# Block attention and two feed-forward stages in fp32 on one core: scores in all four quarters of TensorE, and three parts of w3 @ w_out behind the first x @ w_in

## The chip, the core and the metric

The kernel runs on one core of a Trainium2 chip. A core has TensorE (PE, with its weight loads PEld), VectorE (DVE), ScalarE (ACT), GpSimd (POOL) and SyncE (SP), which here only issues DMAs. The metric is the device time of one execution in microseconds; the number given is the median of several runs. One further execution was taken with the hardware profiler; all rows below are from it.

## What is computed

```python
# attention: batch 2, 8 heads, 768 positions, head size 64; block 32, window 16
k_sum = k.reshape(B, H, nb, block, D).max(axis=3)
v_sum = v.reshape(B, H, nb, block, D).mean(axis=3)
scores_l = where(|i - j| < window, scale * q @ k.T, -1e9)
scores_s = scale * q @ k_sum.T + log(block)
a = softmax(concat([scores_l, scores_s]))
x = a @ concat([v, v_sum])            # then as 1536 x 512
# first feed-forward stage: 512 -> 2048 -> 512
h = x @ w_in
x2 = (h - tanh(h)) @ w_out
# second stage: 512 -> 1024 -> 1024 -> 512
out = (((x2 @ w1) * (x2 @ w2)) @ w3) @ w_out2
```

All inputs and the output are fp32. The weights arrive on the chip as 64-bit numbers.

## The kernel before

**Precision and weights.** The products of the two feed-forward stages are made of three matmuls each (`split_mm`, L176 to L179: high x high, then two with a low half), with operands split into a high and a low half. Class `Weights` (L60) turns each 128x512 block of 64-bit weights ("unit") into such halves: a load by SP (L83), an activation by ScalarE (`start`, L99), three VectorE operations (L102, L104, L106; `dve` issues one of them, `unit` what is left of a unit), a cast by ScalarE (`high`, L134) and a subtraction by GpSimd (`low`, L141). At most three units are between start and `low`. During attention the three VectorE operations work on a PSUM tile `bits` (two buffers), later on the SBUF tile `dec`. Halves live in 15 places that are handed on when a unit has been used up. The matrix w3 @ w_out2 is computed once (32 `w34_part`s of six matmuls, L235; `w34_end`, L250, copies two sums of eight parts from PSUM to SBUF), so that the last stage multiplies by one matrix.

**Attention (L255 to L480).** A head pair (two heads on partitions 0 to 63 and 64 to 127) has 12 tiles of 64 queries; four tiles make a group, three groups a head pair, 24 groups in all. The order on all engines is written by hand: a loop over g = 0 to 27 issues work of up to five groups at once ("iteration g"). `scores(g + 1)` are eight fp32 matmuls 64x64 by 120 columns into one PSUM tile (two buffers). The two heads of a tile go to different halves of rows and of columns. `softmax_a(g, i)` is one VectorE reduction that adds the mask and takes the maximum (L341) and one ScalarE exponential (L344), per tile; `softmax_b(g - 1)` are two small VectorE operations and one GpSimd scaling (L351); `transposes(g - 2)` (L358) go to one PSUM bank, `probs(g - 2)` (L363) copies it to SBUF; `values(g - 3)` (L373) writes one PSUM bank `av`; `x_high(g - 4)` (L384) and `x_low(g - 4)` (L182) read it into the halves of x. `key_blocks` takes the maxima over key blocks on VectorE, and GpSimd writes them between the keys (L299). `value_blocks` (L310) makes the block means of a head pair; SP spreads them by DMA (L320). `busy` (L390) are products of the identity with itself that go nowhere. The number of `w34_part`s in each iteration stands in `N34` (L48). Iterations in `MORE` start two units instead of one.

TensorE's order in one iteration before: scores(g + 1), first part, transposes(g - 2), other parts, values(g - 3). VectorE's: the four reductions, with softmax_b behind the second, x_low behind the third and one decode operation behind each but the first; then a second unit, if one was started, and the key maxima. ScalarE's: x_high, copies of block means, casts of weights, four exponentials, the activation of the next unit, probs, copies of w34_end.

PSUM has eight banks. Attention uses two for scores, two for `bits`, one for transposes, one for `av` and two (`psw`) for w3 @ w_out2.

**First feed-forward stage (L607 to L626).** The loop over n = 0 to 49 issues `hidden(n)` (x @ w_in, 12 matmuls into bank n % 3), then decode work and `curve(n)` (h - tanh(h): for step n - 1 a VectorE select, L517, and ScalarE's cast and GpSimd's subtraction that give gh and gl; for step n four ScalarE and three VectorE operations), then `back(n - 2)` (12 matmuls with w_out into four banks). VectorE does the unit of the step between the select and the products of the curve. The loop before it (`while n34 < 32`) has nothing left to do here. The second stage (L653 on) is untouched.

```python
            for g in range(NG + 4):
...
                if g + 1 < NG:
                    scores(g + 1)
                for i in parts[:1]:
                    w34_part(i)
                if 0 <= g - 2 < NG:
                    transposes(g - 2)
                for i in parts[1:]:
                    w34_part(i)
...
                if 0 <= g - 3 < NG:
                    rest = values(g - 3)
```

Of the kernel before, what the change touches and what calls it, by code (L numbers as in the profile page):

```python
# [19 lines left out]
P = 128  # L20
# [13 lines left out]
TU = 4  # L34
# [13 lines left out]
N34 = [0, 0, 0, 0, 1, 1, 0, 1, 1, 0, 1, 1, 0, 1, 1] + [2] * 13  # L48
# [7 lines left out]
def fused_kernel(tc, qT, kT, vN, vW, w_in, w_out, w1, w2, w3, wo2, out):  # L56
# [3 lines left out]
    class Weights:  # L60
# [26 lines left out]
        def start(self, k=1):  # L87

            for _ in range(k):
# [8 lines left out]
                size = t if self.psum is None else self.psum.tile([P, 512], F32, tag="bits", bufs=2, name=f"bits_{n}")  # L98
# [87 lines left out]
    with tc.tile_pool(name="base", bufs=1) as base, \  # L186
# [68 lines left out]
        with tc.tile_pool(name="p1", bufs=1) as p1, \  # L255
# [66 lines left out]

            def scores(g):
                n, u = divmod(g, NU)
                ps = ps1.tile([P, TU, NC], F32, tag="s", bufs=2, name=f"s_{g}")
                for i in range(TU):
                    t = u * TU + i
                    for hf in range(2):
                        r = slice(hf * QT, (hf + 1) * QT)
                        mm(out=ps[r, i, :], lhsT=qt[n][r, t * QT:(t + 1) * QT], rhs=kt[n][r, t * CW:t * CW + NC],  # L330
                           start=True, stop=True)
                st[g] = ps

            def softmax_a(g, i):
                t = g % NU * TU + i
                mk = masks[0 if t == 0 else 2 if t == NQ - 1 else 1]
                if i == 0:
# [4 lines left out]
                    out=pr[g][:, i, :], in0=st[g][:, i, :], in1=mk[:, :], scale=-0.125, scalar=3.0e38,  # L342
# [23 lines left out]
            def values(g):  # L366
# [3 lines left out]
                for i in range(TU):  # L370
                    for hf in range(2):
                        r = slice(hf * QT, (hf + 1) * QT)
                        mm(out=av[r, i * QT:(i + 1) * QT], lhsT=vg[n][:NC, u * TU + i, r], rhs=sb[:, i, r],  # L373
# [22 lines left out]
            busy(8)  # L396
# [13 lines left out]
            for g in range(NG + 4):  # L410
# [14 lines left out]

                if g + 1 < NG:
                    scores(g + 1)
                for i in parts[:1]:
                    w34_part(i)
                if 0 <= g - 2 < NG:  # L430
                    transposes(g - 2)
                for i in parts[1:]:
                    w34_part(i)
# [17 lines left out]
                for i in range(TU):  # L451
                    if g < NG:
                        softmax_a(g, i)
# [19 lines left out]
            while n34 < 32:  # L473
                wt.start()
                wt.unit()
                w34_part(n34)
                w34_end(n34)
                n34 += 1
                wt.high()
                wt.low()  # L480
        w34_pools.close()
# [3 lines left out]
        psp = ctx.enter_context(tc.tile_pool(name="ps2", bufs=1, space=PSUM, reuse_waits="tile"))  # L485
# [6 lines left out]
        def bank(i, name):  # L492
            return psp.tile([P, TB], F32, tag=f"b{i}", name=name)
# [113 lines left out]
        for n in range(NS + LAG):  # L607
            nxt = hidden(n) if n < NS else None
            if n == NS:
# [12 lines left out]
            wt.low()  # L622
            if not closing:
# [103 lines left out]
```

## Time and profile before

| what | us |
|---|---|
| median of 3 runs | 605.48 |
| lowest and highest run | 603.28, 610.76 |
| the profiled execution | 600.9 |
| its span, first to last instruction | 599.1 |

The mean granted clock of TensorE over the span is 0.995 of full speed. Times in rows are in us from the start of the span unless marked ns. A row of the timeline has the start, the length, the engine, the line, the operation, output<-input with shapes, and how many instructions; in brackets the idle time of the engine before it and what ended that. A row of the busy time by stage has, for each engine, its busy us and the count of instructions, then TensorE's granted clock, the share of the DMA engines and GB/s. Matmuls overlap: a row's length contains the latency of its last matmul, so the time that a group takes is the distance from its start to the start of the next.

### The profile page before, as it was taken

Reading aid. Unit: us, or ns where it says so; the run is one execution under the profiler, and the core shown is the slowest. Engines: PE = TensorE matmul, PEld = TensorE weight load, DVE = VectorE, ACT = ScalarE, POOL = GpSimd, SP = SyncE. Lnnn points to the kernel's source line nnn. Section 1 sums busy time; section 2 is a strip of 40 time slices with the busy share of each in tenths; the row PEclk is TensorE's granted clock in tenths of the full one; section 3 lists DMA queues with packets and bytes.
Section 4 is the critical chain, followed back from the end, with each engine's and each line's share of the span. In section 5 each row is a group of like instructions: output and inputs, shape, how many; then the busy total and the mean of one; then the engine's idle time right before and its main releaser. Section 6 shows DMA issues by size and latency. Waiting matters only on the chain.

```text
span 599.1 us, 8969 instructions
## 1 busy us (share of the span) xinstructions
PE 580.5 (97%) x3216; PEld 469.1 (78%) x3216; DVE 391.8 (65%) x770; ACT 331.3 (55%) x728; POOL 248.0 (41%) x213
## 2 busy tenths in 40 slices
PE   8888999998999999999999999999899999999997
PEld 5666777776888888888888888878688888888885
DVE  3799987799999986679999879999500100010001
ACT  3699887777878864577766667744311211121111
POOL 3466555555566452235555324565632111111110
PEclk9999999998999999999999999999999999999999
DMA  8999986552322320022323002321000100010001
GB/s 310 332 324 321 346 293 207 158 166 105 106 94 85 106 69 0 1 69 73 103 74 106 2 0 73 104 75 67 1 0 1 70 1 0 1 70 1 0 2 70
DMA packets 19676, 59.69 MB, mean 100 GB/s; under 512 B 2096, under 2 KB 4784, under 8 KB 19632
## 3 DMA queue, kind: packets, MB, share of 16 engines
q1 hardware_dynamic: 19632, 59.12, 29.6%
q8 instruction: 25, 0.41, 0.3%
q14 instruction: 19, 0.16, 0.1%
HBM read 54.79 MB, written 3.15 MB: 97 GB/s over the span
## 4 chain that ended last, share of the span: by engine, by line
PE 75%; DVE 13%; issue 4%; DMA 4%; ACT 2%; POOL 1%; SPq 0%; ACTq 0%; DVEq 0%; POOLq 0%
PE x L178 6%; PE x L177 6%; PE x L179 6%; PE ph L177 6%; PE ph L179 6%; PE ph L178 6%; PE w L177 6%; PE w L178 6%; PE w L179 6%; PE o L179 3%; PE o L178 3%; PE o L177 3%; PE busy L394 2%; DVE dec L104 2%; DVE dec L106 2%
## 5 line engine op out<-in xcount | busy, mean ns | idle before, releaser
L141 POOL TENSOR_TENSOR wl<-dec,wh 128x512 fp32r<-128x512 f32 x72 | 111.5, 1552 | 50.2 <-ACT wh L134 43.9
L182 POOL TENSOR_TENSOR gl<-g,gh 128x512 fp32r<-128x512 f32 x48 | 65.1, 1357 | 140.3 <-ACT gh L527 82.3
L590 DVE TENSOR_TENSOR u_a<-u_a,w 128x512 f32<-128x512 f32 x24 | 16.5, 686 | 139.6 <-PE w L179 139.6
L182 POOL TENSOR_TENSOR gl_c<-u_a,gh_c 128x512 fp32r<-128x512 f32 x24 | 31.0, 1290 | 126.9 <-ACT gh_c L592 126.9
L177 PE MATMUL x<-gh,wh 128*128 128x512 f32 x192 | 75.6, 394 | 1.8 <-ACT gh L527 1.8
L178 PE MATMUL x<-gl,wh 128*128 128x512 f32 x192 | 75.7, 394 | 1.6 <-POOL gl L182 1.6
L179 PE MATMUL x<-gh,wl 128*128 128x512 f32 x192 | 75.3, 392 | 0.0
L177 PE MATMUL w<-xh,wh 128*128 128x512 f32 x192 | 75.0, 391 | 0.0
L178 PE MATMUL w<-xl,wh 128*128 128x512 f32 x192 | 75.0, 391 | 0.0
L177 PE MATMUL ph<-xh,wh 128*128 128x512 f32 x192 | 74.8, 390 | 0.0
L179 PE MATMUL w<-xh,wl 128*128 128x512 f32 x192 | 74.7, 389 | 0.0
L179 PE MATMUL ph<-xh,wl 128*128 128x512 f32 x192 | 74.7, 389 | 0.0
L178 PE MATMUL ph<-xl,wh 128*128 128x512 f32 x192 | 74.7, 389 | 0.0
L106 DVE SCALAR_TENSOR_TENSOR dec<-raw,dec 128x512 uint32<-128x512 uint32 x45 | 63.5, 1412 | 1.5
L522 ACT ACTIVATE u<-ph 128x512 f32<-128x512 f32 x48 | 28.8, 600 | 53.1 <-PE ph L179 53.1
L586 ACT COPY u_a<-w 128x512 f32<-128x512 f32 x24 | 14.0, 584 | 73.3 <-PE w L179 73.3
L592 ACT CAST gh_c<-u_a 128x512 fp32r<-128x512 f32 x24 | 14.9, 620 | 71.3 <-DVE u_a L590 71.3
L134 ACT CAST wh<-dec 128x512 fp32r<-128x512 f32 x72 | 44.3, 623 | 12.7 <-DVE dec L106 12.6
L532 DVE TENSOR_TENSOR g<-ph,u 128x512 f32<-128x512 f32 x48 | 32.8, 683 | 19.5 <-ACT th L523 19.4
L517 DVE COPY_PREDICATED g<-mk,th 128x512 f32<-128x512 uint32 x48 | 41.7, 870 | 4.0
L177 PEld LDWEIGHTS x<-gh,wh 128*128 128x128 f32 x192 | 36.3, 189 | 10.2 <-ACT gh L527 2.2
L178 PEld LDWEIGHTS x<-gl,wh 128*128 128x128 f32 x192 | 36.4, 190 | 9.9 <-POOL gl L182 2.3
(90 smaller groups left out, 1270.3 us busy)
## 6 DMA issues: line engine op xcount, KB each, us to landing
raw<-w SPq DMA_DIRECT2D x32, 512.0 KB
raw<-w_in SPq DMA_DIRECT2D x16, 512.0 KB
raw<-w_out SPq DMA_DIRECT2D x16, 512.0 KB
vg<-vW SPq DMA_DIRECT2D x8, 768.0 KB
raw<-wo SPq DMA_DIRECT2D x8, 512.0 KB
kt<-kT SPq DMA_DIRECT2D x7, 544.0 KB
vn<-vN SPq DMA_DIRECT2D x8, 384.0 KB
qt<-qT SPq DMA_DIRECT2D x7, 384.0 KB
```

Source lines behind the costliest of these rows:

```text
L106: lambda tu=tu, su=su, lo=lo: stt(out=tu, in0=lo, scalar=29, in1=su, op0=ALU.logical_shift_right, op1=ALU.bitwise_or)])
L134: nc.scalar.copy(out=h, in_=self.t[n])
L141: nc.gpsimd.tensor_tensor(out=l, in0=self.t[self.n_low], in1=h[:, :].bitcast(F32), op=ALU.subtract)
L177: mm(out=acc, lhsT=lh, rhs=rh, start=start, stop=False)
L178: mm(out=acc, lhsT=lh, rhs=rl, start=False, stop=False)
L179: mm(out=acc, lhsT=ll, rhs=rh, start=False, stop=stop)
L182: eng.tensor_tensor(out=out, in0=x, in1=high.bitcast(F32), op=ALU.subtract)
L517: nc.vector.copy_predicated(out=g, mask=mask[:, :].bitcast(U32), data=t)
L522: nc.scalar.activation(out=u, in_=ph, func=AF.Square)
L532: nc.vector.tensor_tensor(out=gn, in0=ph, in1=u, op=ALU.mult)
L590: nc.vector.tensor_tensor(out=a, in0=a, in1=pb, op=ALU.mult)
L592: nc.scalar.copy(out=ch, in_=a)
```

## The change

The PSUM tile of a group of scores becomes two tiles of half the size, one for the even and one for the odd query tiles, with three buffers. In odd tiles the two heads exchange the output partitions, so that the four matmuls of two neighbouring tiles go to four different quarters of TensorE; `values` reads the probabilities accordingly. The reductions and exponentials go in the order 0, 2, 1, 3. `bits` has one buffer; a second unit started in the same iteration is decoded in SBUF. TensorE's order in an iteration becomes: transposes, all parts, scores, values. Iterations 25 to 27 have 1, 0 and 0 parts (before 2, 2 and 0), and parts 29 to 31 follow `hidden(0)`; their sums are copied after `curve(1)`, and only then is the pool of their two banks closed. These two are banks 2 and 7 of the feed-forward stage. The first run of `busy` has four products instead of eight.

```diff
-N34 = [0, 0, 0, 0, 1, 1, 0, 1, 1, 0, 1, 1, 0, 1, 1] + [2] * 13
+N34 = [0, 0, 0, 0, 1, 1, 0, 1, 1, 0, 1, 1, 0, 1, 1] + [2] * 10 + [1, 0, 0]
...
         def start(self, k=1):
 
-            for _ in range(k):
+            for i in range(k):
...
-                size = t if self.psum is None else self.psum.tile([P, 512], F32, tag="bits", bufs=2, name=f"bits_{n}")
+                size = t if self.psum is None or i else self.psum.tile([P, 512], F32, tag="bits", bufs=1, name=f"bits_{n}")
...
+            def half_of(i, hf):
+
+                hf = (hf + i) % 2
+                return slice(hf * QT, (hf + 1) * QT)
+
             def scores(g):
+
                 n, u = divmod(g, NU)
-                ps = ps1.tile([P, TU, NC], F32, tag="s", bufs=2, name=f"s_{g}")
+                st[g] = [ps1.tile([P, TU // 2, NC], F32, tag="s", bufs=3, name=f"s_{g}_{z}") for z in range(2)]
                 for i in range(TU):
                     t = u * TU + i
                     for hf in range(2):
                         r = slice(hf * QT, (hf + 1) * QT)
-                        mm(out=ps[r, i, :], lhsT=qt[n][r, t * QT:(t + 1) * QT], rhs=kt[n][r, t * CW:t * CW + NC],
-                           start=True, stop=True)
-                st[g] = ps
+                        mm(out=st[g][i % 2][half_of(i, hf), i // 2, :], lhsT=qt[n][r, t * QT:(t + 1) * QT],
+                           rhs=kt[n][r, t * CW:t * CW + NC], start=True, stop=True)
...
-                if i == 0:
+                if g not in nm:
...
-                    out=pr[g][:, i, :], in0=st[g][:, i, :], in1=mk[:, :], scale=-0.125, scalar=3.0e38,
+                    out=pr[g][:, i, :], in0=st[g][i % 2][:, i // 2, :], in1=mk[:, :], scale=-0.125, scalar=3.0e38,
...
-                        mm(out=av[r, i * QT:(i + 1) * QT], lhsT=vg[n][:NC, u * TU + i, r], rhs=sb[:, i, r],
+                        mm(out=av[r, i * QT:(i + 1) * QT], lhsT=vg[n][:NC, u * TU + i, r], rhs=sb[:, i, half_of(i, hf)],
...
-            busy(8)
+            busy(4)
...
+                if 0 <= g - 2 < NG:
+                    transposes(g - 2)
+                for i in parts:
+                    w34_part(i)
                 if g + 1 < NG:
                     scores(g + 1)
-                for i in parts[:1]:
-                    w34_part(i)
-                if 0 <= g - 2 < NG:
-                    transposes(g - 2)
-                for i in parts[1:]:
-                    w34_part(i)
...
-                        softmax_a(g, i)
+                        softmax_a(g, (0, 2, 1, 3)[i])
...
-            while n34 < 32:
-                wt.start()
-                wt.unit()
-                w34_part(n34)
-                w34_end(n34)
-                n34 += 1
-                wt.high()
-                wt.low()
-        w34_pools.close()
...
-        psp = ctx.enter_context(tc.tile_pool(name="ps2", bufs=1, space=PSUM, reuse_waits="tile"))
+        psp = [ctx.enter_context(tc.tile_pool(name="ps2", bufs=1, space=PSUM, reuse_waits="tile"))] * 8
...
-            return psp.tile([P, TB], F32, tag=f"b{i}", name=name)
+            return psp[i].tile([P, TB], F32, tag=f"b{i}", name=name)
...
             nxt = hidden(n) if n < NS else None
+            if n == 0:
+                for i in range(n34, 32):
+                    w34_part(i)
...
             cur = curve(n, nxt, cur)
             wt.low()
+            if n == 1:
+                for i in range(n34, 32):
+                    w34_end(i)
+                w34_pools.close()
+                psp[2] = psp[7] = ctx.enter_context(tc.tile_pool(name="ps3", bufs=1, space=PSUM, side="right",
+                                                                 reuse_waits="tile"))
```

## Rows read from the trace of the kernel before

**Rows 1.** The page's first part: busy us, share and instructions of each engine.

```profile
PE 580.5 (97%) x3216; PEld 469.1 (78%) x3216; DVE 391.8 (65%) x770; ACT 331.3 (55%) x728; POOL 248.0 (41%) x213
```

**Rows 2.** Busy time by stage: start:end, length, then each engine in turn.

```profile
23.00:35.00 12.00, 10.36 (x140) 8.06 (x136) 11.30 (x51) 11.13 (x40) 7.12 (x7) 1.00 0.97 342
69.00:85.00 16.00, 15.66 (x160) 12.13 (x156) 14.29 (x55) 12.69 (x42) 8.40 (x8) 1.00 0.89 291
127.30:137.50 10.20, 8.43 (x39) 6.66 (x37) 9.96 (x14) 7.75 (x16) 3.73 (x3) 1.00 0.56 186
137.50:142.90 5.40, 4.39 (x12) 3.22 (x13) 5.23 (x8) 4.05 (x8) 3.16 (x3) 0.70 0.28 97
148.00:200.00 52.00, 52.00 (x231) 43.06 (x230) 50.42 (x68) 42.17 (x75) 31.04 (x20) 1.00 0.29 93
```

**Rows 3.** TensorE's timeline in iterations 18 and 19.

```profile
89.41 0.69 PE L373 MATMUL av<-pt,vg 120*64 120x64 f32 x16
90.03 0.64 PE L310 MATMUL av<-vn,mean 128*32 128x128 f32 x12
90.59 1.04 PE L330 MATMUL s<-kt,qt 64*64 64x120 f32 x16
91.56 0.50 PE L177 MATMUL w34a<-wh,wh 128*128 128x512 f32 x1
...
93.06 0.60 PE L358 MATMUL t<-ident,pr 128*120 128x128 f32 x4
```

**Rows 4.** TensorE's timeline at the start: busy products, scores 0 and 1, busy products.

```profile
1.36 6.77 PE L394 MATMUL busy<-ident 128*128 128x128 f32 x16 [1.36 <-POOL ident masks.py:199]
8.05 2.77 PE L330 MATMUL s<-kt,qt 64*64 64x120 f32 x32
10.75 4.32 PE L394 MATMUL busy<-ident 128*128 128x128 f32 x16
```

**Rows 5.** Timeline of GpSimd's key blocks and of VectorE's first reductions that waited.

```profile
5.30 0.42 POOL L299 COPY kt<-kb 128x288 f32<-128x288 f32 x1 [0.21 <-DVE kb L298]
10.09 0.28 DVE L341 CUSTOM_DVE_ANT_0 pr<-s,mask 128x120 f32<-128x120 f32 x1 [4.86 <-PE s L330]
22.54 0.28 DVE L341 CUSTOM_DVE_ANT_0 pr<-s,mask 128x120 f32<-128x120 f32 x1 [3.50 <-PE t L358]
33.68 0.28 DVE L341 CUSTOM_DVE_ANT_0 pr<-s,mask 128x120 f32<-128x120 f32 x1 [0.53 <-POOL pr L351]
104.24 0.28 DVE L341 CUSTOM_DVE_ANT_0 pr<-s,mask 128x120 f32<-128x120 f32 x1 [0.90 <-PE t L358]
```

**Rows 6.** Groups by line and shape: count, busy us, mean ns, idle before.

```profile
L106 DVE SCALAR_TENSOR_TENSOR dec<-raw,dec 128x512 uint32<-128x512 uint32 x45 | 63.5, 1412 | 1.5
...
L106 DVE SCALAR_TENSOR_TENSOR dec<-raw,bits 128x512 uint32<-128x512 uint32 x27 | 18.4, 683 | 0.2
...
L99 ACT ACTIVATE bits<-raw 128x512 f32<-128x512 f32 x27 | 16.6, 622 | 0.0
...
L363 ACT COPY pt<-t 120x512 f32<-120x512 f32 x24 | 14.0, 583 | 3.5 <-PE t L358 3.5
```

**Rows 7.** Timeline of the change of stage: values 21 to ph 3.

```profile
119.04 0.69 PE L373 MATMUL av<-pt,vg 120*64 120x64 f32 x16
...
120.18 0.42 DVE L182 TENSOR_TENSOR xl<-av,xh 128x256 fp32r<-128x256 f32 x1 [1.88 <-ACT xh L384]
...
124.94 0.42 DVE L182 TENSOR_TENSOR xl<-av,xh 128x256 fp32r<-128x256 f32 x1
...
137.49 0.50 PE L177 MATMUL x<-gh,wh 128*128 128x512 f32 x1 [1.77 <-ACT gh L527]
...
137.97 0.70 ACT L531 ACTIVATE mk<-u,numax 128x512 f32<-128x512 f32 x1
...
139.01 0.50 PE L178 MATMUL x<-gl,wh 128*128 128x512 f32 x1 [1.01 <-POOL gl L182]
...
143.21 0.40 PE L177 MATMUL ph<-xh,wh 128*128 128x512 f32 x1
```

## The prediction

> **What bounds the kernel now.** I read the page's engine shares first, then the busy time by stage, then the timeline of single stages and the idle time that each wait explains. TensorE has an instruction in flight for 97% of the span [rows 1], but that hides three different regimes [rows 2]. From 23 to 35 us VectorE is busy for 11.30 of 12.00 us and TensorE for 10.36: attention is bound by VectorE (softmax and the decoding of weights). From 69 to 85 us (iterations 15 to 17, two parts of w3 @ w_out in each) TensorE has 15.66 of 16.00 us and VectorE 14.29: TensorE leads by little. From 148 us on TensorE has no gap: 231 matmuls in 52.00 us, 0.225 us each. Between these lies the change of stage: 127.3 to 142.9 us, where TensorE loses 1.8 us and then 1.0 us in front of the first product with w_out, and its granted clock averages 0.70 over 5.40 us [rows 2, 7]. After 148 us a microsecond lost earlier is not won back, so the time moves with the moment at which TensorE starts its dense run. I follow that moment: now it is 143.21 us, where x @ w_in number 3 (I write ph 3) begins [rows 7].
>
> **The scores in four quarters.** I take the distance from the start of one group to the start of the next [rows 3]: 8 score matmuls take 0.97 us (0.121 each, 120 columns, two at a time), 8 value matmuls 0.62 us (0.077 each, 64 columns, two at a time), 6 block-mean matmuls 0.56 us (0.094 each, 128 columns, three at a time). All three fit one line: 0.0016 us for each column streamed, divided by how many run together, plus 0.027 us for each matmul (60, 32 and 43 columns give 0.12, 0.08 and 0.095). With 120/4 = 30 columns a matmul costs 0.074 us and a group 0.59 us, which saves 0.38 us. The ends: nothing saved (0.97 stays) and an exact half (0.48 saved).
>
> The Trainium skill speaks against this: "TensorE: Matmul & The Clock Gate", section "LDWEIGHTS (loading the stationary operand)", gives a weight load its columns divided by 1.2 in ns, as an estimate 53 ns for 64 columns. A score group has 16 such loads, 0.85 us in a row, and only 0.12 us would be saved. The value group also has 16 loads of 64 columns and follows its neighbour after 0.62 us, 0.039 us a load [rows 3], so the trace does not show that floor for loads that go to different column halves; whether it holds between row halves no row shows. It is a rival below.
>
> **The new order in an iteration (b).** The scores come after the transposes and the parts, and with three half-size buffers the odd tiles of the next scores wait for VectorE's first two reductions of the present group; that is why the reductions go 0, 2, 1, 3. Queued behind such a wait are the values, and behind them the next transposes. VectorE reaches those two reductions at once, so this wait costs little. What is new is the place of the transposes: now they stand some 2 us behind their input (a score group and a part lie in front); afterwards they come straight after the values. Their single bank is freed by ScalarE's copy of the iteration before (0.58 us), which follows the weight activation (0.62 us) [rows 6], which with one buffer instead of two waits for the last decode operation of VectorE's iteration. So a loop closes: scores, VectorE's iteration to that operation (about 3.5 us, from 11.30 busy in 12 us over three iterations, less the key maxima), 0.62, 0.58, transposes 0.5 (0.60 with their latency [rows 3]), two parts of six matmuls 2.7, scores 0.59, latency 0.3: 8.8 us for two iterations, 9.4 where a second unit is started. TensorE's own work falls from 15.66 to 14.5 us for three iterations, 4.8 each, VectorE's is 14.29, 4.8 each, the loop 4.4 to 4.7, against 5.33 us now. Three limits this close do not add up smoothly: I expect about 5.1, so 0.25 us in each of the eight iterations 15 to 22, 2.0 us. In iterations 23 to 25 the transposes, now first, wait for GpSimd's two weight subtractions and the scaling of the probabilities; I take 1.0 us off. So b = 1.0 us gained, with the ends 8 x 0.38 = 3.0 gained and 1.0 lost.
>
> In the stage that VectorE bounds, the new place of the transposes frees the probability buffer sooner: now VectorE waits up to 0.53 us for it in every third iteration (33.68 us is the first of three such waits) [rows 5]. **c** = 0.8 us gained, ends 0 and 3 x 0.53 = 1.6. The other 0.38 us per group save nothing here. The second unit of iterations 15, 18 and 21 is decoded in SBUF: the last operation there takes 1.41 us against 0.68 us from PSUM [rows 6], up to 0.7 us for each of three units. VectorE's spare 0.57 us an iteration covers most of it; without that cover it is 2.2 us, and b's lower end holds it. No transfer is added, and SP's order of loads stays as it is.
>
> **Four busy products instead of eight (a).** The first eight take 6.77 us, 0.85 each; the next eight 4.32 us, 0.54 each [rows 4]. Four fewer are 3.4 us, but the scores can't start before GpSimd has written the key blocks at 5.30 + 0.42 = 5.72 us [rows 5], so they start near 5.8 instead of 8.05 us. VectorE's first reduction moves from 10.09 to about 7 us. Its wait of 3.50 us until 22.54 [rows 5] is set by TensorE: scores 1 end near 8.2 us (half of them wait for the reductions), then eight busy products, scores 2 and block means 1.2, eight more busy products, transposes and scores 3 with latency 1.4. With 0.54 us a product that gives 8.2 + 4.3 + 1.2 + 4.3 + 1.4 = 19.4 us, 3.1 us earlier. With 0.85 us through both runs it is 8.2 + 6.8 + 1.2 + 6.8 + 1.4 = 24.4, and slower scores make it 25.0, 2.5 us later. The two groups of scores that take 2.77 us [rows 4] cover the end of the slow stretch now: 1.8 for the first, 0.97 for the second. I take a = 1.5 us gained. VectorE-bound work behind it moves along; the DMA share of 0.97 [rows 2] says that not all of it may.
>
> **Three parts behind the first product (d).** Before, TensorE ends its values 21 near 119.7 us [rows 7], then has transposes, four parts, two value groups and ph 0 to 2, and stands ready at 137.49 - 1.77 = 135.72 us for the product with w_out. That waits for VectorE, which after its wait of 1.88 us at 120.18 us has no other one up to there (9.96 busy of 10.20) [rows 2, 7]: its order (decode units, low halves of x, first curve) is not touched, so an earlier ph 0 does not bring the first curve forward. Afterwards values 23 come two parts and more earlier, but their bank is freed by the low half at 124.94 + 0.42 = 125.4 us. Then 0.6 + 2.7 (ph 0) + 4.05 (18 matmuls) + 2.7 (ph 1) end at 135.4. Now ph 2 needs bank 2, which is the bank of the last w3 @ w_out sum; ScalarE copies it out only behind the curve of step 1, whose last activation ends at 137.97 + 0.70 = 138.67. With a copy of 0.58 (the nearest copy from PSUM) [rows 6] and a semaphore ph 2 starts near 139.4, and ph 3 after 2.7 + 2.7 at 144.8: 1.6 us later than 143.21. TensorE also stands still for some 3.3 us ahead of 125.4 and 4.0 us ahead of 139.4. After such a gap the clock now falls: 5.40 x (1 - 0.70) = 1.6 us lost [rows 2]. If that comes in full, plus 0.4 us of ScalarE delay from its two copies, d is 3.6 us. Ends 1.6 and 3.6 lost, taken 2.6.
>
> **Sum.** 1.5 + 0.8 + 1.0 - 2.6 = 0.7 us gained on the profiled execution's 600.9 us (its span is 599.1, 1.8 us lie around it): 600.2 us. The median of the runs shown is 605.48, 4.6 us above the profiled execution; I keep that distance: 604.8 us. The time in all that follows is on that footing.
>
> **Rivals.** *A, slower:* the slow stretch at the start lasts. It decides at the busy products behind scores 1: 0.85 us apart instead of 0.54, because fewer products and shorter scores lie in front of them. Then a = -2.5, and the same trait in the change of stage makes d 3.6: -2.5 + 0.8 + 1.0 - 3.6 = 4.3 us lost, 609.8. For it: the first eight products alone did not end the stretch [rows 4]. Against: dense scores come 2.2 us earlier.
> *B, faster:* the gap at 137.49 closes, because VectorE gets ahead of TensorE by the waits it has now (0.90 and 1.88 us) [rows 5, 7]. 143.21 - 135.72 - 2.7 = 4.8 us come back, with b = 3.0: 1.5 + 0.8 + 3.0 + 4.8 = 10.1 gained, 595.4. Against: VectorE's unbroken run, and ph 2's new wait on ScalarE.
> *C, the quarters don't run together:* scores stay at 0.97 us, and the new waits stay. b = -1.5, a = 1.0, with c and d as forecast: 2.3 us lost, 607.8. Against: the line through three kinds of matmul. (With the group of 0.85 us that the Trainium skill's page gives above, 8 x 0.12 = 0.9 us less is lost: 606.9.)
>
> **How the numbers follow.** Forecast 0.50, A 0.22, B 0.16, C 0.12. The ends of all four terms together give 6.1 us gained and 7.1 us lost, 599.4 to 612.6 around the median of 605.48. Bad ends rarely all meet, which takes 2 us off above; below, the range reaches towards B: 597.0 to 610.5. A measurement of this kernel tells about 2%, 12.1 us, from no change. Faster than 593.4 is only B with a and c at their best: 0.05. Slower than 617.6 lies past the sum of all bad ends: 0.03. Within 2%: 0.92.
>
> **What would show it.** Score groups 0.59 us long, busy products behind scores 1 at 0.54 us, scores 3 before 22 us, iterations 15 to 22 near 5.1 us, transposes with idle time put down to ScalarE, values 23 waiting for VectorE's low half, ph 2 waiting for ScalarE's copy, and a lowered clock in ph 2. A dense TensorE from ph 0 through the first product with w_out would prove d wrong; iterations of 4.8 us would prove b too small.

## The result, and the profile after

The changed kernel takes 609.96 us (median of 20 runs, 606.46 to 612.53), the kernel before on the same chips 603.08 us (20 runs, 600.33 to 610.76). The ratio is 1.0115 with a 95% interval of 1.010 to 1.013: 6.9 us slower, where 0.7 us faster was forecast. The profiled execution took 611.91 us (span 610.1, mean granted clock 0.986), 11.0 us more than the profiled one of before. Of these 11.0, 4.1 are the choice of executions: before's was 2.2 us under its median, this one 2.0 us above.

The page's first part for the changed kernel; compare [rows 1].

```profile
PE 578.5 (95%) x3208; PEld 465.5 (76%) x3208; DVE 397.0 (65%) x770; ACT 330.3 (54%) x728; POOL 247.8 (41%) x213
```

TensorE is busy for 2 us less and VectorE for 5 us more. The averages say nothing of 7 us, so I follow the moments, as in the prediction. Ph 3 starts at 154.57 us, 11.4 us later than before [rows 7], and from there to the end of the span it is 455.5 us (before 455.9). All of the loss lies ahead of ph 3.

TensorE's timeline at the start of the changed kernel; compare [rows 4].

```profile
1.36 3.36 PE L399 MATMUL busy<-ident 128*128 128x128 f32 x8 [1.36 <-POOL ident masks.py:199]
5.65 1.47 PE L336 MATMUL s<-kt,qt 64*64 64x120 f32 x20 [0.94 <-POOL kt L299]
7.48 1.06 PE L336 MATMUL s<-kt,qt 64*64 64x120 f32 x12 [0.36 <-issue]
8.47 6.77 PE L399 MATMUL busy<-ident 128*128 128x128 f32 x16
...
17.18 6.77 PE L399 MATMUL busy<-ident 128*128 128x128 f32 x16
23.75 1.06 PE L363 MATMUL t<-ident,pr 128*120 128x128 f32 x4
...
27.16 0.69 PE L378 MATMUL av<-pt,vg 120*64 120x64 f32 x16
```

TensorE's values 0 in the kernel before:

```profile
23.88 0.69 PE L373 MATMUL av<-pt,vg 120*64 120x64 f32 x16
```

Scores 0 start at 5.65 us (forecast: near 5.8). But the busy products behind scores 1 stay 0.85 us apart (6.77 us for eight, where before they took 4.32), and so do the next eight; the transposes behind them take 1.06 us, later 0.65. Values 0 start at 27.16 us, before at 23.88: 3.3 us late.

TensorE's timeline in iterations 17 and 18 of the changed kernel; compare [rows 3].

```profile
83.32 0.64 PE L336 MATMUL s<-kt,qt 64*64 64x120 f32 x16
83.89 0.69 PE L378 MATMUL av<-pt,vg 120*64 120x64 f32 x16
84.51 0.65 PE L363 MATMUL t<-ident,pr 128*120 128x128 f32 x4
...
89.83 0.62 PE L363 MATMUL t<-ident,pr 128*120 128x128 f32 x4 [0.71 <-ACT pt L368]
```

A score group takes 83.89 - 83.32 = 0.57 us from start to start (before 0.97). The transposes at 89.83 us wait for ScalarE's copy of the iteration before.

Values 12 and 19 (iterations 15 and 22), first in the kernel before, then in the changed kernel:

```profile
73.42 0.69 PE L373 MATMUL av<-pt,vg 120*64 120x64 f32 x16
...
110.98 0.69 PE L373 MATMUL av<-pt,vg 120*64 120x64 f32 x16
```

```profile
78.79 0.69 PE L378 MATMUL av<-pt,vg 120*64 120x64 f32 x16
...
113.70 0.69 PE L378 MATMUL av<-pt,vg 120*64 120x64 f32 x16
```

From the one to the other it takes 37.56 us before and 34.91 us after.

What TensorE waited for in the changed kernel: engine, line, releaser, us in total, times, longest.

```profile
PE t L363 <- ACT pt L368: 12.3, 14, 2.6
PE av L378 <- DVE xl L182: 4.0, 1, 4.0
PE ph L177 <- ACT w L253: 3.4, 1, 3.4
PE av L378 <- DVE hb L290: 2.2, 1, 2.2
```

None of these four is among the waits of the kernel before, apart from 0.2 us in front of one group of values. Others are gone: TensorE waited 4.2 us for key blocks and 2.5 us for loads of values there, and now 0.9 us for key blocks and not for loads, as far as the profile names them.

Two of the three VectorE reductions that waited from 20 to 55 us; compare [rows 5].

```profile
25.96 0.28 DVE L346 CUSTOM_DVE_ANT_0 pr<-s,mask 128x120 f32<-128x120 f32 x1 [6.71 <-PE s L336]
37.89 0.28 DVE L346 CUSTOM_DVE_ANT_0 pr<-s,mask 128x120 f32<-128x120 f32 x1 [0.48 <-PE s L336]
```

The waits for GpSimd's scaling (0.53 us in the kernel before) are gone, and waits of 0.48 and 0.47 us for the scores stand in their place (the second at 49.37 us). The three reductions are 3.4, 4.2 and 4.2 us later than their counterparts before, at 22.54, 33.68 and 45.19 us.

The change of stage in the changed kernel, TensorE's timeline; compare [rows 7].

```profile
122.60 0.69 PE L378 MATMUL av<-pt,vg 120*64 120x64 f32 x16
...
129.91 1.12 PE L378 MATMUL av<-pt,vg 120*64 120x64 f32 x16 [4.05 <-DVE xl L182]
130.96 0.80 PE L177 MATMUL ph<-xh,wh 128*128 128x512 f32 x1
...
135.78 0.40 PE L177 MATMUL w34a<-wh,wh 128*128 128x512 f32 x1
...
146.16 0.79 PE L177 MATMUL ph<-xh,wh 128*128 128x512 f32 x1 [3.39 <-ACT w L253]
...
154.57 0.39 PE L177 MATMUL ph<-xh,wh 128*128 128x512 f32 x1
```

And ScalarE's there.

```profile
135.98 0.60 ACT L516 ACTIVATE u<-ph 128x512 f32<-128x512 f32 x1 [0.24 <-PE ph L179]
...
142.81 0.60 ACT L516 ACTIVATE u<-ph 128x512 f32<-128x512 f32 x1 [3.46 <-PE ph L179]
...
143.78 0.62 ACT L521 CAST gh<-g 128x512 fp32r<-128x512 f32 x1
...
145.53 1.07 ACT L253 COPY w<-w34a 128x512 f32<-128x512 f32 x2
```

Values 23 stand still for 4.05 us until the low half of x frees their bank. Ph 0 then takes 135.78 - 130.96 = 4.8 us instead of 2.7. Ph 2 stands still for 3.39 us until ScalarE's copies at 145.53 us. ScalarE had to come past the activation u of step 1 first, which waited 3.46 us for ph 1, and ph 1 now lies behind three parts and the slow ph 0. VectorE's last operation on curve 0 had ended at 140.5 us, but the cast that gives gh 0 waits in the same queue to 143.78. This wait costs nothing by itself: the first product with w_out stands behind ph 2 on TensorE and starts at 151.45 us, 0.43 us behind ph 2's last matmul.

The changed kernel's busy time by stage, columns as in [rows 2].

```profile
122.60:131.00 8.40, 4.35 (x60) 3.51 (x59) 7.12 (x10) 4.14 (x8) 4.14 (x3) 0.85 0.42 136
131.00:140.00 9.00, 9.00 (x33) 7.28 (x32) 8.79 (x12) 6.15 (x11) 3.76 (x3) 0.77 0.59 196
140.00:146.20 6.20, 2.81 (x14) 2.00 (x12) 4.48 (x7) 3.39 (x7) 1.72 (x2) 0.94 0.36 127
146.20:154.60 8.40, 8.40 (x25) 6.65 (x26) 5.16 (x8) 4.40 (x9) 2.49 (x2) 0.64 0.17 62
```

From 122.6 to 146.2 us TensorE is idle for 7.4 us, and the granted clock is lowered twice: 0.77 from 131 to 140 us and 0.64 from 146.2 to 154.6 us (0.50 up to 152.2, the lower of its two levels, 1.2 GHz). From values 21 to ph 3 it takes 154.57 - 122.60 = 32.0 us, before 143.21 - 119.04 = 24.2: 7.8 us lost.

### The profile page after: what moved, and what is told of

Same layout as the page of the kernel before. It is cut to its first block, busy times and chain, and to the rows that moved or that the text cites. A ratio compares the mean times of both kernels' runs of the same rounds, so it can differ in the third digit from the quotient of the medians.

```text
span 610.1 us, 9009 instructions
## 1 busy us (share of the span) xinstructions
PE 578.5 (95%) x3208; PEld 465.5 (76%) x3208; DVE 397.0 (65%) x770; ACT 330.3 (54%) x728; POOL 247.8 (41%) x213
## 4 chain that ended last, share of the span: by engine, by line
PE 71%; DVE 16%; issue 8%; ACT 3%; DMA 2%; POOL 0%; SPq 0%; ACTq 0%; DVEq 0%
PE w L177 6%; PE w L178 6%; PE w L179 6%; PE ph L177 6%; PE ph L179 6%; PE ph L178 6%; PE x L177 5%; PE x L178 5%; PE x L179 5%; PE o L179 3%; PE o L178 3%; PE o L177 3%; DVE dec L104 2%; PE busy L399 2%; DVE dec L106 2%
## 5 line engine op out<-in xcount | busy, mean ns | idle before, releaser
L177 PE MATMUL ph<-xh,wh 128*128 128x512 f32 x192 | 76.8, 400 | 3.4 <-ACT w L253 3.4
L179 PE MATMUL ph<-xh,wl 128*128 128x512 f32 x192 | 76.4, 398 | 0.0
L178 PE MATMUL ph<-xl,wh 128*128 128x512 f32 x192 | 76.4, 398 | 0.0
L106 DVE SCALAR_TENSOR_TENSOR dec<-raw,dec 128x512 uint32<-128x512 uint32 x48 | 54.6, 1139 | 1.6
L511 DVE COPY_PREDICATED g<-mk,th 128x512 f32<-128x512 uint32 x48 | 52.6, 1096 | 4.0
L177 PEld LDWEIGHTS ph<-xh,wh 128*128 128x128 f32 x192 | 37.1, 193 | 11.6 <-ACT w L253 3.8
L528 DVE SCALAR_TENSOR_TENSOR g<-sq,g 128x512 f32<-128x512 f32 x48 | 43.4, 904 | 0.6 <-ACT sq L524 0.6
```

Of the source, the lines that this page charges most:

```text
L106: lambda tu=tu, su=su, lo=lo: stt(out=tu, in0=lo, scalar=29, in1=su, op0=ALU.logical_shift_right, op1=ALU.bitwise_or)])
L177: mm(out=acc, lhsT=lh, rhs=rh, start=start, stop=False)
L178: mm(out=acc, lhsT=lh, rhs=rl, start=False, stop=False)
L179: mm(out=acc, lhsT=ll, rhs=rh, start=False, stop=stop)
L511: nc.vector.copy_predicated(out=g, mask=mask[:, :].bitcast(U32), data=t)
L528: nc.vector.scalar_tensor_tensor(out=gn, in0=sq, scalar=GAM, in1=gn, op0=ALU.add, op1=ALU.mult)
```

## The experiments

Each is given as an edit of the changed kernel, unless it says otherwise. Ratios are to the kernel before on the same chip, with a 95% interval.

**The three parts of w3 @ w_out2: e2, e4, e6.** First the old distribution alone is put back.

```diff
-N34 = [0, 0, 0, 0, 1, 1, 0, 1, 1, 0, 1, 1, 0, 1, 1] + [2] * 10 + [1, 0, 0]
+N34 = [0, 0, 0, 0, 1, 1, 0, 1, 1, 0, 1, 1, 0, 1, 1] + [2] * 13
```

> The changed kernel with parts 29 to 31 back in iterations 25 and 26 (only the list of parts per iteration is as before). Theory 1 (the parts behind ph 0 delay ph 1, with it ScalarE's first curve, the cast of gh 0 and the copies that ph 2 waits for): the waits of values 23 and of ph 2 go, ph 3 follows values 21 after 23 to 24 us instead of 32, the time falls by 6 to 8 us against the changed kernel (ratio to before 0.998 to 1.002). Rival (the new order in attention and the start cost the time, the gap in front of the first product with w_out is only moved): falls by less than 2 us (ratio above 1.008).

Measured: 603.10 us, ratio 1.0007 (0.9988 to 1.0027). The 6.9 us are gone, and with them both waits:

```profile
129.34 0.69 PE L378 MATMUL av<-pt,vg 120*64 120x64 f32 x16
129.96 0.50 PE L177 MATMUL ph<-xh,wh 128*128 128x512 f32 x1
...
140.32 0.51 PE L177 MATMUL x<-gh,wh 128*128 128x512 f32 x1 [1.90 <-ACT gh L521]
...
145.87 0.39 PE L177 MATMUL ph<-xh,wh 128*128 128x512 f32 x1
```

This is TensorE's change of stage in e2. Values 23 run without a wait, ph 0 to 2 are dense, and the two waits in front of the product with w_out are those of the kernel before (1.90 and 1.00 us; 1.77 and 1.01 in [rows 7]). From values 21, at 121.84 us, to ph 3 it takes 24.0 us (24.2 in the kernel before, 32.0 in the changed kernel). What is left of the change costs nothing in the median, though the start is as slow as in the changed kernel.

Then the same part alone, on the kernel before: `N34`, the parts behind `hidden(0)`, the copies behind `curve(1)` and the late closing of the pool, all as in the change, with the attention untouched.

```diff
+            if n == 0:
+                for i in range(n34, 32):
+                    w34_part(i)
...
             cur = curve(n, nxt, cur)
             wt.low()
+            if n == 1:
+                for i in range(n34, 32):
+                    w34_end(i)
+                w34_pools.close()
```

> The kernel before with nothing but the three parts behind ph 0 and the later closing of their two banks. Theory 1: values 23 wait for VectorE's low half, ph 2 for ScalarE's copy, the clock is at its lower level in ph 0 and ph 2, and the kernel is 6 to 8 us slower than before (ratio 1.010 to 1.013), nearly the whole difference. Rival (the change of stage costs only because attention ends in another order): less than 3 us slower (ratio below 1.005).

Measured: 609.36 us, ratio 1.0099 (1.0065 to 1.0132). All of TensorE's waits in e4 from 115 to 156 us:

```profile
PE av L373 <- DVE xl L182: 4.0, 1, 4.0
PE ph L177 <- ACT w L253: 3.4, 1, 3.4
```

They are as long as in the changed kernel, 4.0 and 3.4 us. So the loss needs neither the scores in quarters nor the new order.

Last, in the changed kernel, the two copies stand ahead of the curve of step 1 in ScalarE's queue.

```diff
+            if n == 1:
+                for i in range(n34, 32):
+                    w34_end(i)
             cur = curve(n, nxt, cur)
             wt.low()
             if n == 1:
-                for i in range(n34, 32):
-                    w34_end(i)
                 w34_pools.close()
```

> The changed kernel with the two copies of the last w3 @ w_out sums ahead of ScalarE's curve of step 1 (they stood behind it). Theory 1 (the copies, in ScalarE's order behind the activations that wait for ph 1, hold ph 2 back): ph 2 follows ph 1 without a wait, the half-clock stretch in ph 2 goes, the wait of values 23 stays; 4 to 6 us faster than the changed kernel (ratio to before 1.002 to 1.005). Rival (the idle time only moves to the first product with w_out, which waits for gh 0 anyway): the wait in front of that product is 3 to 5 us and the gain is under 2 us (ratio above 1.008).

Measured: 605.57 us, ratio 1.0064 (1.0037 to 1.009), 4.4 us less than the changed kernel. TensorE's wait for the copy is gone and ph 2 follows ph 1 with its matmuls 0.23 us apart; the wait of values 23 for VectorE (4.0 us) and the slow ph 0 stay. By the medians, then, 4.4 of the 6.9 us hang on the place of the copies, and 2.5 on the wait of values 23 and the clock behind it. The split is rough: by the ratios the copies are 3.1 us, and by the profiled executions (32.0, 26.0 and 24.0 us from values 21 to ph 3 in the changed kernel, e6 and e2) 6.0 of 7.9. That the copies are the larger part holds in two of the three.

**Four or eight busy products: e1, e3.** First eight again.

```diff
-            busy(4)
+            busy(8)
```

> The changed kernel with eight busy products at the start again. Theory 1 (the short warm-up costs by itself: values 0 begin 3.3 us later than before): the busy products behind scores 1 come 0.54 us apart, scores 3 begin before 22 us, the time falls by 3 to 5 us against the changed kernel (to about 605 to 607, ratio to the kernel before 1.003 to 1.007). Rival (the start is made up for later, since the middle stage is bound by VectorE and loads): values 0 come earlier but the time stays within 1 us of the changed kernel (ratio 1.010 to 1.013).

Measured: 612.28 us, ratio 1.0163 (1.0139 to 1.0188): 2.3 us slower than with four. TensorE's start in e1:

```profile
10.88 6.77 PE L399 MATMUL busy<-ident 128*128 128x128 f32 x16
...
29.95 0.69 PE L378 MATMUL av<-pt,vg 120*64 120x64 f32 x16
```

With eight products in front the next eight are 0.85 us apart all the same (6.77 us). Four fewer are a gain, and they aren't what keeps the stretch slow.

Then eight again and the old distribution of the parts together.

> The changed kernel with eight busy products and the parts back: what is left is scores in four quarters, the new order, one bits buffer. Theory 1 (the two other edits cost all): 1 to 4 us faster than the kernel before (ratio 0.993 to 0.998). Rival (transposes behind ScalarE's copy cost as much as the quarters give): ratio 0.999 to 1.003, with about 12 us of waits of the transposes for ScalarE's copy as in the changed kernel.

Measured: 606.93 us, ratio 1.0067 (1.0044 to 1.009). Against e2 the eight products cost 3.8 us; against e1 the old distribution of the parts gives 5.4 us. Both expectations miss: e3 is 4.4 us slower than the kernel before. Its start is as slow as e1's (products 0.85 us apart, values 0 at 29.57 us); e8 below shows what that costs.

**The exchange of the heads: e7, e12.** The kernel e3 without the exchange, so that its scores run in two quarters; tiles, buffers and order stay as in the change.

```diff
             def half_of(i, hf):
-                hf = (hf + i) % 2
                 return slice(hf * QT, (hf + 1) * QT)
```

> The kernel with eight busy products, the parts back and the new order, but the heads not exchanged, so that scores use two quarters as before. Theory 2 (at the start the short, interrupted scores in four quarters leave the slow stretch unended; the busy products alone never end it): score groups take 0.97 us again, the busy products behind scores 1 come 0.54 us apart as in the kernel before, values 0 begin near 24.5 us instead of 29.6; in iterations 15 to 22 it loses up to 3 us against the version with quarters, so ratio to before 0.998 to 1.004. Rival (the new order or the wait between the scores ends the warm-up, not the quarters): busy products stay 0.85 us apart, ratio above 1.008.

Measured: 602.99 us (10 runs, 601.95 to 609.66), ratio 1.0017 (0.9991 to 1.0043): less than e3's 606.93, with slower scores. The profiled execution was the one of 609.66 us, and in it the busy products stayed 0.85 us apart and values 0 came at 31.86 us. So the same kernel was run again.

> The kernel e7_two_quarters once more, for a profile of its usual time. Theory (with scores in two quarters the slow stretch ends in scores 0 and 1, as in the kernel before, in most executions; the earlier profile had caught one in which it did not): 603 us, busy products behind scores 1 at 0.54 us, values 0 before 25 us. Rival (the busy products stay 0.85 us apart in its usual executions too, and what gives 603 us comes later): 603 us, but values 0 after 27 us.

Measured: 604.51 us (8 runs), ratio 1.0056 (1.0015 to 1.0096). The runs lie in two groups, five from 602.00 to 605.77 and three from 609.61 to 610.03 us. TensorE's start in the profiled execution of 602.55 us, then in that of e7:

```profile
11.42 4.32 PE L398 MATMUL busy<-ident 128*128 128x128 f32 x16
...
24.40 0.69 PE L377 MATMUL av<-pt,vg 120*64 120x64 f32 x16
```

```profile
11.68 6.77 PE L398 MATMUL busy<-ident 128*128 128x128 f32 x16
...
31.86 0.69 PE L377 MATMUL av<-pt,vg 120*64 120x64 f32 x16
```

One kernel, the same code, and in one execution the products behind scores 1 are 0.54 us apart, in the other 0.85; values 0 come 7.5 us apart, and the times 7.1 us. So with scores in two quarters the slow stretch ends in scores 0 and 1 in some executions; that these are the most is taken from the times, since 14 of the 18 runs of e7 and e12 lie below 606 us and each group has one profile. In all five profiles with scores in four quarters and later products that wait for each other (the changed kernel, e1, e2, e3, e6) it didn't end there. Whether it is the shortness of these scores that counts, or the idle time of 0.35 to 0.41 us inside them, was not tried. Nor is the exchange slower in itself: of two executions with a slow start, e3's reaches ph 3 at 148.59 us and e7's at 151.79.

**Busy products without waits: e8.** Base is e2. The first busy products go to four parts of one tile, so that only every fourth can wait for a bank; the two later runs of eight stay as they are.

```diff
-            def busy(n):
+            def busy(n, close=1):
...
-                    mm(out=w[:, :P], lhsT=ident[:, :], rhs=ident[:, :], start=True, stop=True)
+                    for j in range(close):
+                        mm(out=w[:, j * P:(j + 1) * P], lhsT=ident[:, :], rhs=ident[:, :], start=True, stop=True)
...
-            busy(4)
+            busy(2, 4)
```

> The changed kernel with the parts back, and its first four busy products replaced by eight in two groups of four that write to four slices of one tile, so that none waits for the bank: about the same 3.4 us, but twice the work. Theory 2 (how closely TensorE works at the start decides): the slow stretch ends at or soon behind the first scores, later busy products come 0.54 us apart, values 0 begin 4 to 5 us earlier than with four busy products (near 23 us), 3 to 4 us faster (ratio to before 0.993 to 0.996). Rival (the stretch has a fixed end or needs the long scores): busy products stay 0.85 us apart, ratio 0.999 to 1.002.

Measured: 597.18 us, ratio 0.9911 (0.9862 to 0.996), 5.9 us below e2 and 5.6 us below the kernel before. TensorE's start in e8:

```profile
1.36 4.21 PE L400 MATMUL busy<-ident 128*128 128x128 f32 x16 [1.36 <-POOL ident masks.py:199]
...
7.39 0.63 PE L336 MATMUL s<-kt,qt 64*64 64x120 f32 x12 [0.45 <-issue]
7.95 4.32 PE L400 MATMUL busy<-ident 128*128 128x128 f32 x16
...
21.14 0.69 PE L378 MATMUL av<-pt,vg 120*64 120x64 f32 x16 [1.07 <-DMA raw<-wo]
...
139.14 0.63 PE L177 MATMUL ph<-xh,wh 128*128 128x512 f32 x1
```

Eight products take 4.2 us instead of 6.8 (e1, e3). In the changed kernel the weight loads of the first four products wait three times for the product before, 1.1 us in all; here those of the first eight wait once, 0.4 us. The later ones, which wait for each other as ever, are 0.54 us apart, and values 0 come at 21.14 us, 6.6 us before e2's 27.72. Ph 3 comes 145.87 - 139.14 = 6.7 us before e2's: what the start gains is passed on whole. e3 is the closer comparison, since it differs from e8 in nothing but the waits between the same eight products: 606.93 against 597.18 us, and ph 3 at 148.59 against 139.14.

**No later busy products: e9, e10.** The kernel e2 without the two runs of eight behind scores 1 and 2.

```diff
-                if g < 2:
-                    busy(8)
```

> The changed kernel with the parts back and without the two runs of eight busy products in iterations 0 and 1. Theory 2 (13.5 us of busy products at half speed now stand on the path to transposes 0): values 0 begin before 20 us, real work ends the slow stretch, 4 to 8 us faster than with them (ratio 0.988 to 0.995). Rival (without them the loads and VectorE set the start, or TensorE stays slow into the parts): less than 2 us faster or slower (ratio 0.998 to 1.005), with waits for loads in the first 30 us.

Measured: 597.79 us, 5.3 us below e2, ratio 0.9923 (0.9893 to 0.9952), values 0 at 21.27 us. The time is the theory's, but the stretch isn't ended early: the block means at 22.32 us still take 1.08 us (later 0.64), and values 0 wait 1.18 us for a load. Then both, close products at the start and none later.

> The kernel e8_close without the two later runs of busy products. Theory (the dense products at the start end the slow stretch; the later ones only take TensorE's time, and values 0 then wait for loads): as e8_close and e9, 597 us, values 0 at about 21 us, and no more than 1 us below e8_close. Rival (the two gains, 5.9 us of dense products and 5.3 us of no later ones, have separate causes and add up): 592 us.

Measured: 597.41 us, ratio 0.9907 (0.9877 to 0.9937). The two gains don't add up. TensorE's start in e10:

```profile
13.87 1.18 PE L336 MATMUL s<-kt,qt 64*64 64x120 f32 x16 [3.21 <-POOL kt L299]
18.27 1.08 PE L363 MATMUL t<-ident,pr 128*120 128x128 f32 x4 [3.22 <-ACT pt L368]
...
20.75 1.12 PE L378 MATMUL av<-pt,vg 120*64 120x64 f32 x16 [0.39 <-DMA raw<-wo]
```

At 8.18 us a score group takes 0.56 us, so the slow stretch had ended. Then TensorE waits for key blocks, for copies and for loads, and behind the first of these waits its matmuls are slow again (a score group 1.0 us, granted clock 0.50 from 14 to 20 us), but values 0 come at 20.75 us. So the lowered clock alone isn't what costs at the start: in these runs it costs where 16 products that nobody needs stand in TensorE's queue as well.

**The close products in the kernel before: e11.** The edit of e8 on the kernel before.

> The kernel before, with the first eight busy products written close together into two tiles. Theory (the lower clock at the start comes from busy products that wait for each other, in the kernel before too, but there it ends at about 8 us, in scores 0 and 1): values 0 at about 21.4 instead of 23.88 us, and 2 to 3 us gained, 600.5 us. Rival (the start is hidden behind VectorE and the loads in the kernel before, and only the changed order of TensorE depends on it): within 0.5 us of the kernel before, 603 us.

Measured: 599.32 us, ratio 0.9941 (0.9918 to 0.9964), values 0 at 20.90 us. The kernel before is delayed by its start too, by 3.8 us, more than the 2 to 3 expected. This is most of the 5.6 us by which e8 is below it. What is left for the four quarters and the new order together is the difference between e11 and e8, 2.1 us by the medians and 2.3 us by ph 3 (141.46 and 139.14); the intervals of the ratios overlap, so it isn't shown to be more than noise.

**The order in an iteration: e13.** Base is e10, with the old order: scores, first part, transposes, other parts.

```diff
-                if 0 <= g - 2 < NG:
-                    transposes(g - 2)
-                for i in parts:
-                    w34_part(i)
                 if g + 1 < NG:
                     scores(g + 1)
+                for i in parts[:1]:
+                    w34_part(i)
+                if 0 <= g - 2 < NG:
+                    transposes(g - 2)
+                for i in parts[1:]:
+                    w34_part(i)
```

> The kernel e10_close_alone (scores in four quarters, no busy products behind the first scores) with TensorE's old order in an iteration: scores, first part, transposes, other parts, values. Theory (the new order costs more in the waits of the transposes for ScalarE's copy, 5.6 us from 20 to 60 us and 3.7 us from 60 to 125 us in e10_close_alone, than it gives): these waits are under 1 us, and 2 us are gained, 595.5 us. Rival (it is the new order that makes three iterations 14.9 instead of 16 us from 69 us on, and the shorter scores alone give less): no wait for the copy, three iterations near 15.5 us, 599 us.

Measured: 599.18 us, ratio 0.9932 (0.991 to 0.9955), whose interval overlaps that of e10. The transposes no longer wait, but nothing is gained. From values 12 to values 19 it takes 36.56 us in e13, 34.94 in e10, 34.91 in the changed kernel and 37.56 in the kernel before: of the 2.65 us gained there, 1.0 comes with the shorter scores and their buffers and 1.6 from the new order, by single executions. e7 and e12, with the new order and scores in two quarters, fill the fourth corner: 36.18 us in both, so under the new order the quarters give 1.2 us, and the order with the new buffers 1.4. The rival had said that the order gives this, and 599 us. (Behind ph 3 this profiled execution takes 458.2 us, 2.3 more than the others, with a granted clock of 0.98 from 360 to 460 us; the cause is open.)

## Why the prediction was wrong, and where it was right

**The bound: right.** From ph 3 to the end of the span it is 455.9 us in the kernel before and 455.5 to 456.0 in the changed kernel, e2, e8, e10 and e11. Whatever moved the time moved ph 3.

**The scores: right.** 0.57 us a group, forecast 0.59. Rival C is out. The Trainium skill ("TensorE: Matmul & The Clock Gate", section "LDWEIGHTS (loading the stationary operand)") would give 0.85 us for the 16 loads, an estimate from its formula; the trace disagrees, with 0.57 us for loads and products, 0.036 us a load.

**The new order (b): the step was right, its size too small.** Forecast 2.0 us gained in iterations 15 to 22 and 1.0 lost behind them; measured 2.65 gained from values 12 to 19 and 0.84 lost from 19 to 21. The iterations are 4.99 us (34.91 in seven), forecast 5.1. The loop through ScalarE's copy is there: the transposes wait 14 times, 12.3 us in all, without being late on the whole. The stretch is the same in e2 and e6 (34.93 and 34.91 us). e13 and e7 say that the order gives rather more of it than the scores (1.4 to 1.6 us against 1.0 to 1.2).

**The probability buffer (c): the step failed, its price is open.** The 0.8 us rested on waits that would go and leave nothing behind. They went, and waits for the scores of 0.48 and 0.47 us took their place, so nothing is won there. In addition values 6 waited 2.2 us and the granted clock fell to 0.78 from 50 to 56 us. The lag behind the kernel before is 3.3 us at values 0 and 5.4 us at values 12 (78.79 against 73.42): 2.1 us lost between these two executions, where 0.8 gained were forecast. But this stretch differs between executions. e2 and e6 run the same program as the changed kernel up to there and take 50.3 and 50.0 us for it, the changed kernel 51.6; e4, with the attention of the kernel before, takes 50.5, the kernel before 49.5. So neither a gain nor a loss is shown. The profile puts the wait of values 6 down to a VectorE operation. In e2 (the line below) and e6 the same values wait 1.3 and 1.4 us for a load, so I take it for that load, coming later still; it wasn't tried.

```profile
52.67 1.11 PE L378 MATMUL av<-pt,vg 120*64 120x64 f32 x16 [1.28 <-DMA qt<-qT]
```

**The start (a): wrong in the sum, the price that of rival A, but not its reason.** That the scores start near 5.8 us was right. The step that failed is that the busy products behind scores 1 run 0.54 us apart: they stay at 0.85, and 1.5 us gained became 3.3 lost (values 0 at 27.16, in e2 and e6 at 27.72 and 27.86; 23.88 in the kernel before and 24.41 in e4). Rival A had this with 2.5 us. It gave "fewer products and shorter scores" as the cause, and half of that fell: with eight products the stretch lasts as well (e1), and the four fewer gain 2.3 us (e1 against the changed kernel) to 3.8 us (e3 against e2). The scores in four quarters are the half that stands: without the exchange most executions are at the kernel before's time (e7, e12). Of why the stretch ends in one execution and not in another, only this is shown: the products are longer apart where they wait for each other, and eight that don't wait end it (e8 against e3).

**The three parts (d): mis-sized by a factor of three, and this alone is the loss.** Forecast 2.6 us, end 3.6; measured 7.8 us between the profiled executions, 6.9 between the medians with and without it, 6.8 alone on the kernel before. The waits were named: values 23 for the low half of x, ph 2 for ScalarE's copy, a fallen clock. Two steps failed. The first is "ScalarE copies it out only behind the curve of step 1, whose last activation ends at 138.67": that time was kept from the kernel before, though the curve's own input, ph 1, had been moved behind three parts. ScalarE ran its instructions in the written order, so u waited 3.46 us, and the copies behind it came late with it; with the copies ahead of u TensorE's wait was gone (e6). The second is that I charged the clock once, with 1.6 us: it fell behind both gaps, and ph 0 takes 4.8 us instead of 2.7 (2.1 lost) and the 14 matmuls from ph 2 on 0.43 us each instead of 0.225 (2.9 lost). Taken from values 21 on, my working put ph 2 at 139.4 and ph 3 at 144.8; shifted by the 3.6 us that values 21 are late these are 143.0 and 148.4, and it came to 146.16 (3.2 late) and 154.57 (6.2 late). e6 tells the two gaps apart: 4.4 us for the copy, 2.5 for values 23, by the medians.

**The sum.** By the profiled executions: start 3.3 lost, then 2.1 lost, 1.8 gained from values 12 to 21, 7.8 lost, 11.4 together, which is the shift of ph 3. The last two terms come back in other executions (43.8 us from values 12 to 21 in e2 and e6, 45.6 in e4; 30.9 and 31.0 us from values 21 to ph 3 in e4 and e1). Of the 3.6 us by which values 21 are late, part belongs to the two executions compared: values 21 start at 122.60, 121.84 and 121.67 us in the changed kernel, e2 and e6, and at 119.04 and 120.57 in the kernel before and e4; by the medians e2, which has all of the change but (d), loses nothing. The measured 609.96 us lies inside the forecast's 597.0 to 610.5 by luck, since that range stands on 605.48 us; from 603.08 its upper end would be 608.1. Rival A's 609.8 us is near the measured 609.96, but by other terms, and from a footing of 605.48 us (three runs) where 20 runs give 603.08: its 4.3 us lost are fewer than the 6.9 measured. Rival B needed VectorE to get ahead by the waits that it has before; it never did.

## What to carry to other kernels

When work is moved behind another product, shift every time that depends on that product, also on engines whose own order isn't touched: a copy that an engine runs behind other work is as late as the latest input of anything ahead of it (here 3.4 us of waiting on TensorE). Price each gap on TensorE twice, as the wait and as the matmuls behind it at the lower clock (here behind gaps of 4.0 and 3.4 us). Products that only keep TensorE busy should not wait for one another, and shouldn't stand in front of work that is due: here either was worth 5 to 6 us in the changed kernel with its parts back, nearly as much as the change lost, and the first 3.8 us in the kernel before. e8 and e10 (597.2 and 597.4 us) beat both kernels, by their start more than by the change.

## What the runs showed of the hardware

At the start the column of the granted clock does not show what the durations show. The busy time from 23.5 to 26.5 us, first in the changed kernel, then in e10:

```profile
23.50:26.50 3.00, 3.00 (x28) 2.19 (x29) 0.54 (x5) 1.32 (x3) 0.47 (x1) 1.00 0.93 311
```

```profile
23.50:26.50 3.00, 3.00 (x19) 2.28 (x20) 2.80 (x7) 3.00 (x11) 2.34 (x3) 0.64 0.99 389
```

The four transposes in or next to this stretch take 1.06 us in the changed kernel (at 23.75) and 1.08 us in e10 (at 23.13), later 0.65 in both; the column says 1.00 and 0.64. In e10 it fits: it is 0.50 from 14 us to 25.3, where the transposes take 1.08 us and the matmuls of a part come 0.43 us apart, and 0.23 apart behind. In the changed kernel it is 1.00 from the start on, through all of the slow stretch. So the start is read from the distances of the products, and that they mean the lower clock there is taken from the same durations in e10. How long it stays slow also differs between executions of one kernel, which moved the time by 7 us in e7 and e12; two of the 20 runs of the kernel before lie at 610.3 and 610.8 us, and four of the changed kernel's at 606.5 to 607.5 with the others at 609.2 or more, but of these there is no profile.
